# Attention and two mixture layers on one core: half of the strided loads from a second queue

## The chip, the cores and the metric

One core of a Trainium2 chip runs the program. The metric is the device time of one launch in microseconds (us). Before the change the median of three runs is 638.58 us (638.17 to 639.22). A difference under about 0.2% of that, 1.28 us, can't be told from no change here.

## The reference

Three steps, all in float32:

```python
# 1. attention: batch 4, 8 heads, 576 positions, 64 per head
scores = q @ k.T / 8
local   (heads 0-3): rel >= 0 and rel < 32
strided (heads 4-7): rel >= 0 and pos_k % 32 == pos_q % 32
x = softmax(where(mask, scores, -1e9)) @ v         # -> 2304 tokens x 512
# 2. each token goes to the one of 8 experts with the largest cosine:
#    out = gate * (relu(x @ w1[e]) @ w2[e])          (512 -> 1024 -> 512)
# 3. y = max(x @ w1, x @ w2, x @ w3) @ w_out         (512 -> 768 -> 512)
```

## The kernel before

The program is written out in one order by hand; every engine works through its own list, and waits stand on semaphores. The first 124 us are the attention, which also routes the tokens; the remaining 512 us are the experts and the last layer, which TensorE bounds.

The attention takes its work in 44 groups, 11 for each batch: five local groups (kind 0), then six strided ones (kind 1). A strided group is a piece `j` (0 to 2) and a half `hh` (0 or 1), in the order (0,0), (0,1), (1,0), and so on. The strided queries and keys lie in the tiles `qs` and `ks` of 128 partitions x 2 halves x 2 x 576. Half 0 has its data in partitions 0 to 63, half 1 in partitions 64 to 127; the other partitions of each half hold codes that build the mask and are written once, in `setup`. So a group of half 0 needs the loads of partitions 0 to 63 alone, and one of half 1 those of 64 to 127.

The loop in `attention` is a software pipeline over steps `s`. In step `s` the scores of group `s` are issued (`g_scores`, L386), the maximum and the exponentials of group `s-1` (`g_max` L393, `g_exp` L405), the division of group `s-2` (`g_norm`, L417 on GpSimd), the transposes of group `s-4` (L425, copied out by VectorE in L427), a projection of 128 tokens (`tok_half`, L479, copied to `row` in L487 or L489), and the product with the values of group `s-5` (L444, copied out by ScalarE in L454, which the next step issues first). Scores have three buffers in PSUM: group `s` can start when the exponentials of group `s-3` are done.

All loads of the attention are issued by SyncE, one after the other, and SyncE waits where a tile is still being read. Queries and keys of the next kind are asked for by `load_kq` in step 0 or 5 of a batch's 11, the values by `load_v` in steps 4 and 10. For the second to fourth batch the strided ones are asked for at `s` = 11, 22 and 33, when the last strided group of the batch before has been issued; their first group is five steps later, at `s` = 16, 27 and 38. Stores of finished tokens (`x_scr`, L492) go through the same SyncE queue, and so do the weights of the last layer that are re-packed on the way (`c_load`, L213).

Each DMA raises one of eight semaphores, DMAHW0 to DMAHW7, taken in turn. A DMA also waits until the one that used its semaphore before has landed, so at most eight are under way.

Of the kernel before, what the change touches and what calls it, by code (L numbers as in the profile page):

```python
# [69 lines left out]
def kernel(ctx, tc, a, out, x_scr, w_scr, u_scr, perm_scr, gate_scr, upto="all"):  # L70
    nc = tc.nc
# [237 lines left out]
    qs = pa.tile([128, 2, 2, S], F32, name="qs")  # L309
    ks = pa.tile([128, 2, 2, S], F32, name="ks")  # L310
# [14 lines left out]
    def load_kq(b, kind, cuts):  # L325

        for c0, c1, n0, n1 in cuts:
            if kind == 0:
                k0 = n0 + 32 * (n0 > 0)
                nc.sync.dma_start(out=kl[:, c0:c1, k0:n1 + 32], in_=a["ktl"][b][:, c0:c1, k0:n1 + 32])  # L330
                nc.sync.dma_start(out=ql[:, c0:c1, 2 * n0:2 * n1], in_=a["ql"][b][:, c0:c1, 2 * n0:2 * n1])
            else:
                for hh in range(2):
                    h = slice(64 * hh, 64 * hh + 64)
                    nc.sync.dma_start(out=ks[h, hh, c0:c1, n0:n1], in_=a["kts"][b, h, c0:c1, n0:n1])
                    nc.sync.dma_start(out=qs[h, hh, c0:c1, n0:n1], in_=a["qs"][b, h, c0:c1, n0:n1])

    def load_v(b, kind, cuts=((0, 4),)):
        if (b, kind) not in vv:
# [320 lines left out]
    def setup():  # L660
        nc.sync.dma_start(out=masks, in_=a["masks"])
        nc.vector.memset(junk[:, 0:256], 0.0)
        warm(W0, junk)

        nc.scalar.activation(out=junk[:, 1:2], in_=junk[:, 0:1], func=ACTF.Exp)
        for hh, h in enumerate((slice(64, 128), slice(0, 64))):
            for u, (t, eng) in enumerate(((qs, CODE[hh]), (ks, CODE[2 + hh]))):
                shape = [64, 2, 32, 18]
                (nc.gpsimd if eng else nc.vector).tensor_tensor(
                    out=t[h, hh].rearrange("p c (r s) -> p c r s", r=32), op=ALU.add,  # L670
                    in0=bc(code_r[h, u].unsqueeze(1).unsqueeze(3), shape), in1=bc(code_s[h, u].unsqueeze(1).unsqueeze(1), shape))
        load_kq(0, 0, ((0, 1, 0, 256), (0, 1, 256, S), (1, 2, 0, S)))
        nc.sync.dma_start(out=cf, in_=a["cf"][:, 0:308])
        load_v(0, 0, ((0, 2),))
        load_kq(0, 1, ((0, 2, 0, 252),))
        load_v(0, 0, ((2, 4),))
        load_kq(0, 1, ((0, 2, 252, S),))
        nc.sync.dma_start(out=ca, in_=a["cf"][:, 308:])
        nc.sync.dma_start(out=em, in_=a["emb"])
        nc.sync.dma_start(out=tau_c, in_=a["tau"])  # L680
        nc.sync.dma_start(out=cb, in_=a["cb"])
# [544 lines left out]
    with tc.If(over > 0):  # L1226
# [23 lines left out]
        with tc.For_i(0, 16 * E, 1) as j:  # L1250
            val = nc.values_load(tabs[0][0:1, bass.ds(j, 1)], min_val=0, max_val=1)
            with tc.If(val > 0):
# [11 lines left out]
                    out=g, out_offset=None, in_=x_scr, in_offset=bass.IndirectOffsetOnAxis(ap=ids[:, 0:1], axis=0))  # L1264
# [18 lines left out]
                for f in range(6):  # L1283
                    for m in range(3):
                        ps = fpsum("fm")
                        for c in range(4):
                            o = 256 * c + 128 * (f % 2)
                            nc.tensor.matmul(
                                out=ps[:, 0:128], lhsT=wm[:, 3 * (f // 2) + m, o:o + 128], rhs=y2[:, c], start=c == 0, stop=c == 3)
# [5 lines left out]
                for f in range(6):  # L1295
# [5 lines left out]
                    out=out, out_offset=bass.IndirectOffsetOnAxis(ap=ids[:, 0:1], axis=0), in_=fo, in_offset=None)  # L1301
# [89 lines left out]
```

## Time and profile before

| | us |
|---|---|
| median of 3 runs | 638.58 |
| the profiled execution | 638.13 |
| its span, first to last instruction | 636.4 |
| TensorE busy | 610.5 (96%) |
| VectorE busy | 448.9 (71%) |
| ScalarE busy | 336.9 (53%) |
| GpSimd busy | 138.6 (22%) |
| DMA | 130.81 MB, mean 206 GB/s |

A busy engine is not by that the bound: the table is an average over the attention and the two layers, which differ. What a load in the attention is worth has to be read there, from the waits at the groups that use it.

### The profile page before, as it was taken

The page shows a single profiled execution, that of the slowest core. Times are in us where ns is not written, and L with a number is a line of the kernel's source. Part 1 is how long each engine was busy: PE and PEld are TensorE (multiplying, and loading weights), DVE is VectorE, ACT ScalarE, POOL GpSimd, SP SyncE. Part 2 cuts the span into 40 slices and gives each one's busy share as a digit, 9 for nine tenths or more (in the row PEclk, how much of TensorE's full clock was granted, in tenths as well). Part 3 has the DMA queues.
Part 4 walks back from the last instruction along what each step waited for, and adds up shares of the span by engine and source line. Part 5 has one row for each costly group of instructions (what it writes and reads, how often), then busy time and mean ns, then how long its engine had stood idle before and what let it go on. Part 6 is the DMA issues. An engine that isn't in the chain of part 4 may idle for free.

```text
span 636.4 us, 11933 instructions
## 1 busy us (share of the span) xinstructions
PE 610.5 (96%) x4281; PEld 575.7 (90%) x4282; DVE 448.9 (71%) x1011; ACT 336.9 (53%) x909; POOL 138.6 (22%) x133
## 2 busy tenths in 40 slices
PE   7889998799999999999999999999999999999995
PEld 6788887589999999999998999988999988999984
DVE  6868988576899798979899978777344375335440
ACT  3668777555675656566765635546322256221242
POOL 5424443345414142323210000002000012000021
PEclk7999999799999999999999999999999999999998
DMA  8998772584989596878774875931376301377011
GB/s 222 295 227 225 224 195 67 163 285 149 332 285 332 200 347 209 279 239 270 269 249 132 309 305 202 370 154 59 109 268 233 116 33 61 132 269 264 38 49 54
DMA packets 44881, 130.81 MB, mean 206 GB/s; under 512 B 4633, under 2 KB 15513, under 8 KB 41457
## 3 DMA queue, kind: packets, MB, share of 16 engines
q1 hardware_dynamic: 41792, 120.50, 57.1%
q0 software_dynamic: 3024, 9.49, 4.0%
q8 instruction: 36, 0.59, 0.4%
q14 instruction: 29, 0.23, 0.1%
HBM read 97.73 MB, written 32.24 MB: 204 GB/s over the span
## 4 chain that ended last, share of the span: by engine, by line
PE 82%; DVE 7%; DMA 7%; issue 1%; SPq 1%; ACT 1%; POOL 0%; POOLq 0%; DVEq 0%; ACTq 0%
PE g L833 63%; PE q L833 10%; DMA qs<-qs 3%; PE s L386 2%; PE x L444 2%; PE r L479 2%; PE q L816 1%; DMA ks<-kts 1%; DMA out<-r,perm_i 1%; PE t L425 1%; DMA em<-emb 1%; DVE pt L427 1%; DVE mx L393 1%; DMA xg<-x_scr,win_i 1%; DVE tmp L1118 1%
## 5 line engine op out<-in xcount | busy, mean ns | idle before, releaser
L833 PE MATMUL g<-xc,w 128*128 128x384 f32 x1134 | 198.0, 334 | 0.0
L833 PEld LDWEIGHTS g<-xc,w 128*128 128x128 f32 x1134 | 196.5, 188 | 1.2 <-ACT yt L1131 0.5
L178 DVE TENSOR_TENSOR w<-stage,w 128x1024 fp32r<-128x1024 f32 x76 | 104.5, 1391 | 16.5 <-ACT w L173 15.9
L833 PE MATMUL g<-h,w 128*128 128x376 f32 (+7 forms) x768 | 111.6, 301 | 1.5 <-DVE h L853 1.5
L833 PEld LDWEIGHTS g<-h,w 128*128 128x128 f32 x768 | 104.6, 189 | 2.4 <-DVE h L853 1.8
L833 PE MATMUL g<-xw,w 128*128 128x376 f32 (+7 forms) x768 | 106.0, 298 | 0.5 <-ACT xw L808 0.3
L833 PEld LDWEIGHTS g<-xw,w 128*128 128x128 f32 x768 | 104.3, 189 | 0.9 <-ACT xw L808 0.6
L173 ACT ACTIVATE w<-stage 128x1024 fp32r<-128x1024 f32 x76 | 78.7, 1055 | 6.5 <-DMA stage<-w 5.7
L1182 POOL DMA_INDIRECT out<-r,perm_i x18 | 17.9, 994 | 279.3 <-ACT r L1181 197.0
L833 PE MATMUL q<-w,hs 128*128 128x512 f32 x324 | 74.8, 390 | 1.3 <-DVE hs L1170 1.3
L833 PEld LDWEIGHTS q<-w,hs 128*128 128x128 f32 x324 | 60.6, 188 | 14.8 <-DVE hs L1170 2.6
L405 ACT ACTIVATE p<-s,nb 128x96 f32<-128x96 f32 (+2 forms) x152 | 50.7, 346 | 21.7 <-DVE r L414 16.4
L249 POOL TENSOR_TENSOR f<-f,c 128x512 int32<-128x512 int32 x24 | 35.0, 1460 | 108.7 <-DVE f L247 94.4
L1131 ACT ACTIVATE yt<-g 128x384 f32<-128x384 f32 x27 | 13.3, 491 | 72.8 <-PE g L833 40.1
L1118 DVE TENSOR_TENSOR tmp<-g,yt 128x384 f32<-128x384 f32 x36 | 20.0, 555 | 44.7 <-PE g L833 44.7
L417 POOL TENSOR_TENSOR p<-p,ri 128x384 f32<-128x384 f32 (+3 forms) x44 | 36.0, 818 | 60.3 <-DVE ri L416 47.1
L852 ACT ACTIVATE h<-g 128x376 fp32r<-128x376 f32 (+7 forms) x64 | 25.7, 410 | 29.9 <-PE g L833 27.8
L971 DVE TENSOR_TENSOR xc<-yt,xc 128x384 fp32r<-128x384 f32 x42 | 21.4, 553 | 16.4 <-ACT xc L970 16.4
L867 ACT ACTIVATE yt<-g 128x376 f32<-128x376 f32 (+7 forms) x32 | 13.3, 414 | 37.0 <-PE g L833 37.0
L427 DVE COPY pt<-t 96x512 f32<-96x512 f32 (+3 forms) x44 | 25.5, 580 | 8.9 <-PE t L425 8.8
L797 POOL DMA_INDIRECT xg<-x_scr,win_i x22 | 25.8, 1173 | 23.5 <-PE q L947 11.4
L405 ACT ACTIVATION_READ_ACCUMULATOR p<-s,nb 128x1 f32 (+2 forms) x152 | 30.9, 203 | 0.0
(175 smaller groups left out, 793.6 us busy)
## 6 DMA issues: line engine op xcount, KB each, us to landing
stage<-w SPq DMA_DIRECT2D x64, 512.0 KB
c<-wm SPq DMA_DIRECT2D x24, 512.0 KB
w<-u_scr SPq DMA_DIRECT2D x12, 1024.0 KB
u_scr<-w SPq DMA_DIRECT2D x9, 1024.0 KB
w<-u_scr SPq DMA_DIRECT2D x12, 768.0 KB
u_scr<-w SPq DMA_DIRECT2D x9, 768.0 KB
w_scr<-f SPq DMA_DIRECT2D x24, 256.0 KB
stage<-w_scr SPq DMA_DIRECT2D x12, 512.0 KB
```

What stands on the lines that cost most here:

```text
L173: nc.scalar.activation(out=ws[i][:, 0, 0:m], in_=x, func=ACTF.Copy)
L178: nc.vector.tensor_tensor(out=ws[i][:, 1, 0:m], in0=x, in1=ws[i][:, 0, 0:m].bitcast(F32), op=ALU.subtract)
L249: nc.gpsimd.tensor_tensor(out=f, in0=f, in1=low, op=ALU.add)
L405: nc.scalar.activation(out=p[:nq, i, :nk], in_=st[g]["ps"][:nq, i * nk:(i + 1) * nk], func=ACTF.Exp, bias=st[g]["nb"][:nq, i:i + 1], scale ...
L417: nc.gpsimd.tensor_tensor(out=d["p"][:nq, 0:ns, :nk], in0=d["p"][:nq, 0:ns, :nk], in1=ri[:nq, 0:ns].to_broadcast([nq, ns, nk]), op=ALU.mult)
L427: nc.vector.tensor_copy(out=pts[:nk, 0:ns, :nq], in_=pt[:nk, 0:ns * nq].rearrange("p (s q) -> p s q", s=ns))
L797: nc.gpsimd.indirect_dma_start(out=t[i][:r], out_offset=None, in_=x_scr, in_offset=bass.IndirectOffsetOnAxis(ap=win_i[:r, NWIN * e + i:NWI ...
L833: nc.tensor.matmul(out=ps, lhsT=ws(i), rhs=xs(j), start=first and n == 0, stop=last and n == 2, skip_group_check=more)
L852: nc.scalar.activation(out=h[:, 0], in_=ps, func=ACTF.Relu)
L971: nc.vector.tensor_tensor(out=x[:, 1], in0=src[c], in1=x[:, 0].bitcast(F32), op=ALU.subtract)
L1118: nc.vector.tensor_tensor(out=tmps[i], in0=ps, in1=s, op=ALU.add)
L1182: nc.gpsimd.indirect_dma_start(out=out, out_offset=bass.IndirectOffsetOnAxis(ap=perm_i[:, col:col + 1], axis=0), in_=r, in_offset=None)
```

## The change

In the strided branch of `load_kq` the two loops change places, so that both halves of the keys are issued before both halves of the queries. For the second to the fourth batch (`b` above 0) the half of partitions 64 to 127 is issued by ScalarE, in ScalarE's list at the place where `load_kq` is called; the half of partitions 0 to 63 stays with SyncE. For the first batch SyncE issues all four, in the new order. The tiles, the bytes and the shapes of the transfers are the same.

```diff
             else:
-                for hh in range(2):
-                    h = slice(64 * hh, 64 * hh + 64)
-                    nc.sync.dma_start(out=ks[h, hh, c0:c1, n0:n1], in_=a["kts"][b, h, c0:c1, n0:n1])
-                    nc.sync.dma_start(out=qs[h, hh, c0:c1, n0:n1], in_=a["qs"][b, h, c0:c1, n0:n1])
+                for t, x in ((ks, "kts"), (qs, "qs")):
+                    for hh, queue in enumerate((nc.sync, nc.scalar if b else nc.sync)):
+                        h = slice(64 * hh, 64 * hh + 64)
+                        queue.dma_start(out=t[h, hh, c0:c1, n0:n1], in_=a[x][b, h, c0:c1, n0:n1])
```

SyncE's list around the load of the second batch, before. `c` is a weight to re-pack, `v<-vl` the local values, `v<-vs` the strided values, `kl` and `ql` the local keys and queries of the third batch; in brackets the semaphores that are waited for.

```order
L213 DMA c<-wm 128x1024 [waits DMAHW2_49]
L342 DMA v<-vl 96x2304 [waits DMAHW3_49]
L335 DMA ks<-kts 64x1152 [waits DMAHW4_49,PE_49]
L336 DMA qs<-qs 64x1152 [waits DMAHW5_49]
L335 DMA ks<-kts 64x1152 [waits DMAHW6_49,PE_49]
L336 DMA qs<-qs 64x1152 [waits DMAHW7_49]
L342 DMA v<-vs 126x1280 [waits DMAHW0_49]
L330 DMA kl<-ktl 128x1216 [waits DMAHW1_49,PE_49]
```

The first `ks` and `qs` are half 0, the second two half 1. The same stretch of SyncE now:

```order
L213 DMA c<-wm 128x1024 [waits DMAHW2_49]
L342 DMA v<-vl 96x2304 [waits DMAHW4_49]
L336 DMA ks<-kts 64x1152 [waits DMAHW6_49,PE_49]
L336 DMA qs<-qs 64x1152 [waits DMAHW7_49]
L342 DMA v<-vs 126x1280 [waits DMAHW0_49]
L330 DMA kl<-ktl 128x1216 [waits DMAHW1_49,PE_49]
```

The loads of half 0 keep their place behind `c` and `v`; those of half 1 are gone from here. ScalarE's list at the same step, as the difference of the two kernels (`p` are the exponentials, `xt` the copied product with the values):

```order
 L454 ACTIVATE xt<-x 128x128
 L405 ACTIVATE p,rs<-s,nb 72x72 x4
+L336 DMA ks<-kts 64x1152
+L336 DMA qs<-qs 64x1152
 L454 ACTIVATE xt<-x 128x2x14x18
 L405 ACTIVATE p,rs<-s,nb 128x96 x8
```

ScalarE now issues the two loads of half 1 behind the exponentials of the last strided group of the batch before (72x72) and ahead of the next copy `xt`. The same at the third batch:

```order
 L515 ACTIVATE junk,ssq<-row 128x512
 L405 ACTIVATE p,rs<-s,nb 72x72 x2
+L336 DMA ks<-kts 64x1152
+L336 DMA qs<-qs 64x1152
 L515 ACTIVATE junk,ssq<-row 128x512
 L454 ACTIVATE xt<-x 128x2x14x18
```

Here a sum of squares for the routing (L515) and the copy `xt` stand behind the two issues. SyncE in the first batch, second cut of the positions, before:

```order
L342 DMA v<-vl 96x1152 [waits DMAHW5_49]
L335 DMA ks<-kts 64x2x324 [waits DMAHW6_49]
L336 DMA qs<-qs 64x2x324 [waits DMAHW7_49]
L335 DMA ks<-kts 64x2x324 [waits DMAHW0_49]
L336 DMA qs<-qs 64x2x324 [waits DMAHW1_49]
L678 DMA ca<-cf 128x40 [waits DMAHW2_49]
```

In the changed kernel these rows read `ks`, `ks`, `qs`, `qs` with the same waits in the same order: the queries of half 0 move from the second place to the third. TensorE's, VectorE's and GpSimd's lists are unchanged.

## Rows read from the trace of the kernel before

**Rows 1.** The page's part 4, shares of the chain that ended last.

```profile
PE 82%; DVE 7%; DMA 7%; issue 1%; SPq 1%; ACT 1%; POOL 0%; POOLq 0%; DVEq 0%; ACTq 0%
PE g L833 63%; PE q L833 10%; DMA qs<-qs 3%; PE s L386 2%; PE x L444 2%; PE r L479 2%; PE q L816 1%; DMA ks<-kts 1%; DMA out<-r,perm_i 1%; PE t L425 1%; DMA em<-emb 1%; DVE pt L427 1%; DVE mx L393 1%; DMA xg<-x_scr,win_i 1%; DVE tmp L1118 1%
```

**Rows 2.** The chain of waits, 20 to 50 us: start, length, what.

```profile
28.38 16.06 DMA qs<-qs
44.57 1.11 PE s L386 x8
```

**Rows 3.** Windows by stage: us, then busy and (count) per engine, PEclk, DMA share, GB/s.

```profile
44.57:64.00 19.43, 19.43 (x224) 17.63 (x225) 15.77 (x58) 16.03 (x74) 8.37 (x11) 1.00 0.88 242
64.00:124.00 60.00, 52.86 (x607) 45.84 (x607) 51.26 (x204) 43.79 (x191) 21.39 (x27) 0.97 0.55 151
```

**Rows 4.** Timeline, second batch's strided loads and their first two groups: start, length, engine.

```profile
28.38 0.59 SPq L336 DMA_DIRECT2D qs<-qs  x1
29.74 0.35 SPq L342 DMA_DIRECT2D v<-vs  x1
31.38 0.30 ACT L405 ACTIVATE p<-s,nb 72x72 f32<-72x72 f32 x1
32.86 1.05 ACT L454 ACTIVATE xt<-x 128x504 f32<-128x504 f32 x1 [1.08 <-PE x L444]
39.34 0.35 ACT L405 ACTIVATE p<-s,nb 128x96 f32<-128x96 f32 x1
41.63 1.11 PE L386 MATMUL s<-ks,qs 128*126 128x126 f32 x8 [1.48 <-ACT xt L454]
44.57 1.11 PE L386 MATMUL s<-ks,qs 128*126 128x126 f32 x8 [0.31 <-DMA qs<-qs]
```

**Rows 5.** Windows by which transfers are under way, columns as in rows 3.

```profile
25.00:26.00 1.00, 1.00 (x22) 0.76 (x20) 0.68 (x3) 1.00 (x7) 0.83 (x1) 1.00 1.05 440
29.00:30.00 1.00, 0.91 (x7) 0.79 (x8) 0.93 (x6) 0.49 (x4) 0.10 (x1) 1.00 1.02 412
40.00:41.00 1.00, 0.15 (x6) 0.00 (x1) 0.98 (x3) 1.00 (x7) 0.63 (x1) 1.00 0.94 194
42.00:43.00 1.00, 1.00 (x11) 1.00 (x11) 0.00 (x0) 0.14 (x2) 0.79 (x1) 1.00 0.92 212
53.61:65.77 12.16, 12.16 (x133) 10.91 (x131) 10.34 (x45) 10.23 (x47) 5.05 (x8) 1.00 0.95 219
80.19:90.35 10.16, 10.16 (x112) 9.10 (x111) 8.55 (x31) 8.89 (x39) 4.12 (x7) 1.00 0.96 224
```

**Rows 6.** Timeline, third batch: values issued, ScalarE's list, first strided group.

```profile
53.61 0.62 SPq L342 DMA_DIRECT2D v<-vl  x1
57.32 0.31 ACT L405 ACTIVATE p<-s,nb 72x72 f32<-72x72 f32 x1
60.96 0.34 ACT L405 ACTIVATE p<-s,nb 128x96 f32<-128x96 f32 x1 [0.54 <-DVE r L414]
65.77 1.14 PE L386 MATMUL s<-ks,qs 128*126 128x126 f32 x8
```

**Rows 7.** Timeline, fourth batch, the same places and VectorE's copy of a transpose.

```profile
80.19 0.62 SPq L342 DMA_DIRECT2D v<-vl  x1
86.79 0.34 ACT L405 ACTIVATE p<-s,nb 128x96 f32<-128x96 f32 x1 [1.15 <-DVE r L414]
90.35 1.14 PE L386 MATMUL s<-ks,qs 128*126 128x126 f32 x8
91.87 0.61 PE L425 MATMUL t<-cf,p 128*96 128x128 f32 x4 [0.38 <-POOL p L417]
93.64 0.66 DVE L427 COPY pt<-t 96x512 f32<-96x512 f32 x1
```

**Rows 8.** Timeline, first batch: second cut's first strided group, and the next idle time.

```profile
20.17 1.11 PE L386 MATMUL s<-ks,qs 128*126 128x126 f32 x8 [0.25 <-DMA qs<-qs]
23.27 0.69 PE L444 MATMUL x<-pt,v 96*64 96x64 f32 x16 [1.55 <-ACT xt L454]
```

## The prediction

> **What bounds the kernel now.** I read the chain of waits first. TensorE has 82% of it and the DMAs 7%; 73% is line 833, the layers behind the attention [rows 1], which the change does not touch. What the change can move lies in the attention, and one piece there is a load of it: the strided queries of the second batch, issued at 28.38, hold the chain for 16.06 us, until 44.44, and the scores at 44.57 start on that landing [rows 2]. From there to 64 us TensorE is busy 19.43 of 19.43 us [rows 3], so whatever is late at 44.57 is late at 64. From 64 to 124 us VectorE is the fullest of the engines beside TensorE (51.26 and 52.86 of 60 us), and the two feed each other; a delay of one is absorbed only where the other has work in hand.
>
> Then the timeline at the two groups. The first strided group of the second batch (half 0) starts at 41.63 after 1.48 us of idle TensorE [rows 4]. The view names a ScalarE copy, but a score needs no copy: it needs its buffer, which the exponentials of three groups earlier, ended with the row at 39.34, had freed, and its loads. So I take this wait for the landing of half 0, about 41.6. The second group (half 1) starts at 44.57 after only 0.31 us idle, on the landing at 44.44. Between the two lie 2.63 us of TensorE work. The loads thus land one after the other, half 0 first, in the order in which the two groups want them.
>
> Last the windows. While 128-partition loads are under way the queue moves 412 to 440 GB/s; while those of 64 partitions and the values are, 194 to 212; the DMA share is 0.92 to 1.05 in both [rows 5]. The engines of the DMA are busy all the time in either case; in the second they take twice as long for the same bytes.
>
> **The change part by part.**
>
> *The second batch.* SyncE's own issues hardly move: half 0 stays behind the weights and the local values in its queue, and that queue is backlogged. What is new is when half 1 starts. ScalarE reaches its two issues behind the exponentials at 31.38, about 31.8 us, and its queue is empty, so half 1 is served at once, beside the local values that are still in SyncE's queue. Before, 0.59 MB of half 1 (2 transfers of 64 x 1152 x 4 bytes) ran behind half 0; now they run ahead of most of it. If the rate of the two queues together is the 194 to 212 GB/s of the row, the four transfers end when they ended before, but half 0 ends last: at 44.44 in place of 41.6. The first group waits 2.8 us longer. The second finds its data there and follows after the 2.63 us of work: 44.55 + 2.63 = 47.2 in place of 44.57. Cost 2.6 us, all on the path. From the other side: if half 1 slows SyncE's queue not at all, half 0 lands at 41.6 as before and the second group loses its 0.31 us of waiting, a gain of 0.3. The ends are −0.3 and +2.6. I take 2.6, since the nearest rows have the DMA share at 0.92 to 1.05 at the low rate: no DMA engine stands idle that a second queue could put to work.
>
> A rule of the Trainium skill is on the side of that choice. The page "SBUF — State Buffer", section "Can I just issue two DMAs to hit both halves?", says that two concurrent transfers, one at partition 0 and one at partition 64, came to only 6% more than one. No run here shows two such queues yet. By that rule the two pairs of transfers, 2.8 us each, would together take 0.3 us less, and the cost here would be 2.3 in place of 2.6.
>
> *The third batch.* SyncE is held by the token stores until 53.61 and then issues the local values [rows 6]. The last store (0.26 MB), the values (0.88 MB) and half 0 (0.59 MB) are 1.74 MB, at 219 GB/s [rows 5] 7.9 us: half 0 lands near 61.5 and is wanted at 65.77. ScalarE issues half 1 at about 57.8, behind the exponentials at 57.32. Shared rates push half 0 back by its partner's 0.59 MB, 2.7 us, to 64.2, still ahead of the group. The count is a mean over 16 DMA engines, and the last of them ends later, so some wait can appear: 0 to 1.1 us, I take 0.3.
>
> *The fourth batch.* The same count from 80.19 at 224 GB/s gives half 0 at 88.0, and with half 1 ahead of it 90.6; the group starts at 90.35 now [rows 7]. So it waits at least 0.25 and, with a slow last engine, up to 2.6 us. Of that VectorE hides a part: it takes up the transpose of 91.87, ended at 92.48, only at 93.64, so it has 1.16 us of work in hand. Between 0 and 1.5 us reach the path; I take 0.5.
>
> *ScalarE's time.* An issue of such a load takes 0.59 us on SyncE [rows 4], so the pair is about 1.2 us of ScalarE. In the second batch this lies in a gap of 1.08 us, ahead of the copy at 32.86, which waits for TensorE. In the third ScalarE has no gap until 60.96 (0.54 us), in the fourth until 86.79 (1.15 us), and the sum of squares, the copy `xt` and the next exponentials are queued behind the pair; VectorE waits for those exponentials, TensorE's next product for the copy. Cost 0 to 1.2 in each of the two; I take 0.2 each, 0.4 together, since the gap follows within two groups. Would those gaps not be there, it would be 2.4. The new waits of the two loads on earlier DMAs cost nothing: the corresponding loads of SyncE stood behind landings of the same age and were issued by 28.38, before ScalarE arrives.
>
> *The first batch.* The new order puts the queries of half 0 one issue later in each cut. The group at 20.17 already waits 0.25 us for them [rows 8] and will wait about 0.9 longer, one transfer of 0.17 MB at 200 GB/s. It costs nothing, because TensorE is idle 1.55 us before 23.27 anyway, for a copy on ScalarE that stands behind the load of the expert vectors; without that cover it would be the 0.9.
>
> Sum against the profiled execution: 638.13 + 2.6 + 0.3 + 0.5 + 0.4 + 0 = 641.9 us. That execution is 0.45 us under the median of the three runs, well within 0.2%.
>
> **The rivals.**
>
> *The halves help each other.* The 64-partition loads may be slow because their half of the partitions takes no more, and not because the DMA engines are full; then half 1 from a second queue uses the idle other half and SyncE's transfers keep their pace. For it: the same share of busy time at half the rate [rows 5], which says that each packet is slowed at its target. Against it: nothing in the trace shows two queues at work in the attention. Then half 0 lands at 41.6, half 1 long before its group, and the third and fourth batch lose nothing; with ScalarE's issues hidden in its gaps the time is 638.13 − 0.3 = 637.8, not slower. It decides as soon as the two queues together move over about 350 GB/s while both are under way. The Trainium skill, page "SBUF — State Buffer", section "Door 1: The DMA port swizzle", has partitions 0 to 63 and 64 to 127 on different ports, which would be its ground; no row here shows ports.
>
> *Half of that.* If both together move about 300 GB/s, half 1 is done in some 4 us, in which SyncE's queue loses about 1.3 us: half 0 lands at 42.9, a cost of 1.0; the third batch 0, the fourth 0.1, ScalarE 0.2: 639.4.
>
> *ScalarE is the price.* The transfers hide, but each pair of issues falls on the path: 3 x 1.2 = 3.6 us, 641.7. For it: ScalarE is busy 16.03 of 19.43 us [rows 3]. Against it: the gaps named above. The time is near the forecast's, so the place must tell them apart: a late `xt` rather than a late first group.
>
> **How the numbers follow.** Forecast 0.55; the halves help each other 0.20; half of that 0.14; ScalarE's price 0.06; a gain that I can't derive, from a shifted pattern of waits, 0.05. What a measurement here can tell from no change is about 0.2%, 1.28 us, so slower begins at 639.4. Slower: 0.53 of the forecast's 0.55, 0.07 of the half case's 0.14 and 0.06: 0.66. Same: 0.20 + 0.07 + 0.02 = 0.29. Faster 0.05. The forecast's own range is 639.8 to 645.3: the second batch at 1.7, with the rest at 0; and all upper ends together but ScalarE's, 2.8 + 1.1 + 1.5, with 1.8 of ScalarE's 2.4. With the helping case in it the range is 637.5 to 645.
>
> **What would show it.** Right: the first strided group of the second batch starts near 44.5 with some 4 us of idle TensorE ahead of it, the second group has no wait for a load, and the DMA rate from 33 to 44 us stays near 200 GB/s. Wrong: that group still starts near 41.6, or the rate in that stretch exceeds 300, or the copies `xt` behind the new issues start over 1 us late with TensorE idle for them. A time under 639.4 would refute the step of the second batch.

## The result and the profile after

The changed kernel takes 642.32 us (median of 22 runs), the kernel before 639.26 us (22 runs): a ratio of 1.0053, 95% interval 1.0035 to 1.0071, so 3.4 us slower (2.2 to 4.5). The profiled execution of the changed kernel took 646.22 us, 3.9 above its own median. Its attention is some 3 us late; another 5 us come after the attention, where TensorE has the work of before. Single runs of the kernel before differ by as much (637.5 to 642.6 us), so I compare places in the attention and leave the rest to the medians.

First the chain that ended last. Its pieces in the second batch (start, length, what) say which transfer holds it [rows 2]:

```profile
25.66 17.20 DMA qs<-qs
42.86 0.14 issue
42.99 1.61 PE s L386 x8
```

The transfer on the chain was the queries of half 1; now it is those of half 0, issued by SyncE at 25.66 and landed at 42.86. The scores behind it take 1.61 us, before 1.11. The timeline of the same place, ScalarE's rows first, then TensorE's [rows 4]:

```profile
29.14 0.55 ACTq L336 DMA_DIRECT2D ks<-kts  x1
29.81 0.52 ACTq L336 DMA_DIRECT2D qs<-qs  x1
31.54 1.06 ACT L454 ACTIVATE xt<-x 128x504 f32<-128x504 f32 x1 [1.85 <-PE x L444]
...
37.38 0.61 PE L386 MATMUL s<-kl,ql 128*128 128x96 f32 x4
42.99 1.61 PE L386 MATMUL s<-ks,qs 128*126 128x126 f32 x8 [4.16 <-DMA qs<-qs]
47.15 1.14 PE L386 MATMUL s<-ks,qs 128*126 128x126 f32 x8
```

ScalarE's two issues fit into its gap: the next copy `xt` waits for TensorE. The first strided group waits 4.16 us in place of 1.48, the second not at all. From group to group it is 4.16 us, though the work between them took 2.63 before. The windows of the changed kernel (us, busy and count per engine, PEclk, DMA share, GB/s) show why [rows 5]:

```profile
33.00:44.00 11.00, 6.84 (x71) 6.22 (x70) 6.05 (x22) 6.60 (x36) 3.31 (x4) 0.98 1.01 201
40.00:41.00 1.00, 0.00 (x0) 0.00 (x0) 0.35 (x2) 0.81 (x5) 0.36 (x1) 1.00 1.07 237
44.00:45.00 1.00, 1.00 (x6) 0.98 (x6) 0.00 (x0) 0.00 (x0) 0.00 (x0) 0.50 0.95 225
46.00:47.00 1.00, 1.00 (x18) 0.75 (x17) 0.97 (x4) 0.00 (x0) 0.00 (x0) 0.57 0.95 397
```

and the first of these stretches in the kernel before:

```profile
33.00:44.00 11.00, 9.52 (x106) 8.77 (x106) 7.26 (x26) 7.92 (x39) 3.73 (x5) 1.00 0.99 195
```

Two readings. With two queues the DMAs move 201 GB/s where one moved 195, at a share of 1.0 in both: a second queue brings no more that can be told. (The same stretch has 196 to 205 GB/s in six profiles that load half of the second batch from ScalarE, this one and five from below, and 195 to 239 in six that load all of it from SyncE; the 3% lie far inside that spread.) And after the 4.16 us without work TensorE's granted clock is 0.50, the level of 1.2 GHz, until it is back near 47 us: that is the long work between the groups, 4.16 − 2.63 = 1.5 us.

When half 1 moves can be read too. Of the DMA queues q10 appears only in kernels in which ScalarE loads; q1 is SyncE's. The first row below is the stretch from 34 to 36 us, the next two that from 36 to 42 (packets, MB, share of the 16 engines), the last the time from issue to landing of ScalarE's queries:

```profile
q10 hardware_dynamic: 2, 0.01, 2.6%
...
q1 hardware_dynamic: 160, 0.71, 55.1%
q10 hardware_dynamic: 150, 0.58, 44.5%
...
qs<-qs ACTq DMA_DIRECT2D x1, 288.0 KB, 14.1
```

ScalarE issues at 29.14 and 29.81, but from 30 to 34 us q10 moves nothing; nearly all of half 1's 0.59 MB goes from 36 to 42, side by side with SyncE's bytes. Its queries land at 29.81 + 14.1 = 43.9, a microsecond behind half 0's 42.86. TensorE reaches the second group only at 47.15, so it finds them there.

From 47 to 67 us TensorE is again busy throughout, as in [rows 3], so nothing of the delay is given back:

```profile
47.15:66.60 19.45, 19.45 (x228) 17.66 (x225) 15.55 (x55) 16.20 (x74) 8.16 (x11) 1.00 0.68 180
```

The third and fourth batch: ScalarE's first issue and the second strided group of the third, then the first two of the fourth [rows 6, 7]:

```profile
59.76 0.48 ACTq L336 DMA_DIRECT2D ks<-kts  x1
...
72.01 1.11 PE L386 MATMUL s<-ks,qs 128*126 128x126 f32 x8 [0.21 <-DMA qs<-qs]
...
94.10 1.11 PE L386 MATMUL s<-ks,qs 128*126 128x126 f32 x8 [0.87 <-issue]
96.89 1.15 PE L386 MATMUL s<-ks,qs 128*126 128x126 f32 x8
```

The second group of each batch is the clean place to compare, since the waits of the first lie ahead of it. In the kernel before, the last local group ahead of the second batch's and the second groups of the third and fourth batch:

```profile
38.70 0.61 PE L386 MATMUL s<-kl,ql 128*128 128x96 f32 x4
...
69.11 1.15 PE L386 MATMUL s<-ks,qs 128*126 128x126 f32 x8
...
94.03 1.14 PE L386 MATMUL s<-ks,qs 128*126 128x126 f32 x8
```

Before, the second groups started at 44.57, 69.11 and 94.03; now they start 2.58, 2.90 and 2.86 us later. Nearly all of the attention's delay arises in the second batch, in this execution.

### The profile page after: what moved, and what is told of

It reads as the page before. It is cut to its first block, busy times and chain, and to the rows that moved or that the text cites. A ratio compares the mean times of both kernels' runs of the same rounds, so it can differ in the third digit from the quotient of the medians.

```text
span 644.4 us, 11937 instructions
## 1 busy us (share of the span) xinstructions
PE 613.0 (95%) x4281; PEld 577.4 (90%) x4282; DVE 449.2 (70%) x1011; ACT 337.6 (52%) x909; POOL 138.1 (21%) x133
## 4 chain that ended last, share of the span: by engine, by line
PE 77%; DMA 11%; DVE 9%; issue 1%; ACT 1%; SPq 0%; POOL 0%; POOLq 0%; DVEq 0%; ACTq 0%
PE g L833 59%; PE q L833 10%; DMA qs<-qs 4%; PE s L386 2%; PE r L479 1%; PE q L816 1%; DMA cf<-cf 1%; PE x L444 1%; DMA out<-r,perm_i 1%; DMA kl<-ktl 1%; DMA ks<-kts 1%; DVE pt L427 1%; DMA xg<-x_scr,win_i 1%; DVE w L178 1%; DMA stage<-w 1%
## 5 line engine op out<-in xcount | busy, mean ns | idle before, releaser
L833 PE MATMUL g<-h,w 128*128 128x376 f32 (+7 forms) x768 | 113.4, 304 | 1.5 <-DVE h L853 1.5
L833 PEld LDWEIGHTS g<-h,w 128*128 128x128 f32 x768 | 106.3, 192 | 2.7 <-DVE h L853 2.0
L405 ACT ACTIVATE p<-s,nb 128x96 f32<-128x96 f32 (+2 forms) x152 | 50.7, 348 | 19.2 <-DVE r L414 14.1
```

The lines of the kernel that those rows point to most:

```text
L405: nc.scalar.activation(out=p[:nq, i, :nk], in_=st[g]["ps"][:nq, i * nk:(i + 1) * nk], func=ACTF.Exp, bias=st[g]["nb"][:nq, i:i + 1], scale ...
L833: nc.tensor.matmul(out=ps, lhsT=ws(i), rhs=xs(j), start=first and n == 0, stop=last and n == 2, skip_group_check=more)
```

## The experiments

My theory: the second queue brings no more bytes, half 0 lands late, TensorE waits, and its clock falls on top. The rivals: ScalarE's issues are the price; the first batch's new order is what matters; every batch pays. All ratios are to the kernel before, run on the same chip in turn.

| kernel | ratio | 95% interval |
|---|---|---|
| new order in the first batch only | 0.9963 | 0.9940 to 0.9987 |
| second batch only | 1.0036 | 1.0007 to 1.0066 |
| third and fourth only | 1.0077 | 1.0046 to 1.0109 |
| halves swapped between the queues | 1.0116 | 1.0080 to 1.0153 |
| ScalarE's issues, without the bytes | 1.0023 | 0.9994 to 1.0051 |
| new order, one queue | 1.0005 | 0.9976 to 1.0034 |
| changed kernel, 14 filling products | 1.0082 | 1.0048 to 1.0116 |
| third batch only | 1.0088 | 1.0058 to 1.0117 |
| first and second batch | 1.0042 | 1.0014 to 1.0070 |
| third only, ScalarE's queue used earlier | 1.0018 | 0.9991 to 1.0044 |
| changed kernel, 6 filling products | 1.0043 | 1.0013 to 1.0073 |
| first batch only, re-packing later | 0.9995 | 0.9976 to 1.0014 |

In the diffs, `new(b)` stands for the changed loop, `old` for that of before.

**The parts, each alone.**

```diff
-new(b) for every b
+new(b) if b == 0 else old
```

> The new order of the four loads (keys of both halves, then queries of both halves) in the first batch alone, all from SyncE; batches two to four as before. The prediction put this at nothing: 0 us against the kernel before. Rival: the changed kernel's profile is 2.1 us early at the load of the expert vectors and 1.3 us early at 40 us, and if the new order is the cause this kernel is 1 to 2 us faster than before (ratio 0.997 to 0.9985) and its first strided group of the second batch starts near 40.3.

Measured: 0.9963, about 2.4 us faster, against my 0. Two more kernels below have the same order in the first batch, and they show 1.0005 and 0.9995. One interval of three excludes no change; I take the gain as not settled.

```diff
-new(b) for every b
+new(b) if b == 1 else old
```

> ScalarE issues half 1 in the second batch alone; first, third and fourth batch as before. Theory of the late half 0: the whole cost is here, +3 to +4.3 us (ratio 1.005 to 1.007), the first strided group of the second batch starts near 44.5 after about 4 us of idle TensorE. Rival, the issues on ScalarE are the price: a third of the cost, +1 us, with that group near 41.6.

Measured: 1.0036, 2.3 us. The first two strided groups of the second batch:

```profile
41.35 1.11 PE L386 MATMUL s<-ks,qs 128*126 128x126 f32 x8 [1.09 <-DMA qs<-qs]
45.51 1.11 PE L386 MATMUL s<-ks,qs 128*126 128x126 f32 x8 [1.53 <-DMA qs<-qs]
```

Here half 0 costs no more than before (1.09 us of waiting, before 1.48) and half 1 is late: the second group starts 0.94 us later than before. ScalarE reached its issues at 31.33 in this execution, in the changed kernel's at 29.14. So one of the halves is late here too, but the other one; that this goes with ScalarE's later start is my reading, and no run varies it alone.

```diff
-new(b) for every b
+new(b) if b > 1 else old
```

> ScalarE issues half 1 in the third and fourth batch alone; first and second batch as before. Theory of the late half 0 in the second batch: no cost, -0.3 to +0.5 us (ratio 0.9995 to 1.0008). The prediction's own terms for these batches are +1.2 us. Rival, ScalarE's issues: two thirds of the cost, +2 us (ratio 1.003).

Measured: 1.0077, 4.9 us. My theory of these two batches missed by far. ScalarE's first issue, and TensorE's first two strided groups of the fourth batch:

```profile
56.20 3.41 ACTq L336 DMA_DIRECT2D ks<-kts  x1
```

```profile
93.85 2.04 PE L386 MATMUL s<-ks,qs 128*126 128x126 f32 x8 [1.75 <-DMA qs<-qs]
98.02 1.14 PE L386 MATMUL s<-ks,qs 128*126 128x126 f32 x8
```

An issue that took 0.48 us in the changed kernel takes 3.41 here, with the sum of squares and the copy `xt` queued behind it. In the fourth batch half 0 is late by 1.75 us, and the group's 8 products take 2.04 us in place of 1.14, at the lower clock. The second groups of this execution's second and third batch:

```profile
43.54 1.18 PE L386 MATMUL s<-ks,qs 128*126 128x126 f32 x8 [0.45 <-DMA qs<-qs]
...
70.84 1.14 PE L386 MATMUL s<-ks,qs 128*126 128x126 f32 x8
```

It enters the third batch 1.03 us ahead of the kernel before (43.54 against 44.57). From second group to second group it takes 27.30 us (before 24.54), and to that of the fourth 27.18 (before 24.92): losses of 2.8 and 2.3 us, 5.0 together, as the medians have it.

**The halves change queues.**

```diff
-SyncE loads half 0, ScalarE half 1
+SyncE loads half 1, ScalarE half 0   (b > 0; b == 0: old)
```

> As the change for batches two to four, but with the halves exchanged: ScalarE issues half 0, which the first strided group needs, SyncE half 1; the first batch in the old order. Theory of the late half: half 0 lands by 40 us, the first strided group of the second batch starts without a wait near 40.2, half 1 lands near 44.4 as before and the second group starts near 44.6 after about 1.8 us of idle TensorE; no cost, -0.5 to +0.5 us (ratio 0.999 to 1.001). Rival, ScalarE's issues or a slower rate of two queues together: +3 us as the change (ratio 1.005).

Measured: 1.0116, 7.4 us, against no loss. The first two strided groups of the second and of the third batch:

```profile
45.08 2.04 PE L386 MATMUL s<-ks,qs 128*126 128x126 f32 x8 [3.44 <-DMA qs<-qs]
49.87 1.43 PE L386 MATMUL s<-ks,qs 128*126 128x126 f32 x8
...
75.32 2.04 PE L386 MATMUL s<-ks,qs 128*126 128x126 f32 x8 [3.88 <-DMA qs<-qs]
80.10 1.66 PE L386 MATMUL s<-ks,qs 128*126 128x126 f32 x8
```

ScalarE's queue starts later than SyncE's (30.08 against 26.71 for the second batch's first issue), and now it carries the half that is wanted first. Both batches wait 3.4 to 3.9 us for it, and in both the clock falls behind the wait: from group to group it is 4.8 us (before 2.9 in the second batch, 3.3 in the third). The profiled execution, 650.49 us, is the slowest of six, so its places show the kind of loss and not its size.

**ScalarE's issues without the bytes.**

```diff
 SyncE: old, but half 1 without its last 16 positions (b > 0)
+ScalarE: ks and qs of half 1, last 16 of 576 positions, where new(b) issues
```

> The loads keep the order and the queue they had before, but the last 16 of the 576 positions of half 1 are loaded by ScalarE, at the places where the change puts its loads: six more issues on ScalarE, almost no bytes in its queue. It asks which part of the change's loss is ScalarE's time. If the loss of the third and fourth batch (4.9 us when these alone were changed) is made of ScalarE's issues, this kernel loses it too, and some of it in the second batch: 3 to 6 us, a ratio of 1.005 to 1.009. If the loss is made of half 0 landing later, because half 1 runs beside it, this kernel loses the 0 to 1.2 us of three pairs of issues: a ratio of 1.000 to 1.002. I expect 1.001.

Measured: 1.0023, an interval that holds 0 and the 1.2 us of the issues, and whose upper end, 3.3 us, is nearly the change's whole loss. The ratio alone doesn't settle it; the trace says more. The first strided groups of the second, third and fourth batch (this kernel's line numbers are three higher):

```profile
40.30 1.11 PE L389 MATMUL s<-ks,qs 128*126 128x126 f32 x8 [0.30 <-DMA qs<-qs]
...
64.44 1.14 PE L389 MATMUL s<-ks,qs 128*126 128x126 f32 x8
...
89.01 1.14 PE L389 MATMUL s<-ks,qs 128*126 128x126 f32 x8
```

They lie 1.33, 1.33 and 1.34 us ahead of those before (41.63, 65.77, 90.35). The lead doesn't shrink over the second and third pair of issues. The first pair, at 31.09 and 31.83, lies ahead of these groups: the local groups on either side of it start at 29.73 and 38.56, before at 29.82 and 38.70, so it costs nothing either, and the lead comes from a load that landed earlier (a wait of 0.30 us in place of 1.48). On the path the issues cost nothing in this execution.

**The new order in one queue.**

```diff
-for hh, queue in enumerate((nc.sync, nc.scalar if b else nc.sync)):
+for hh, queue in enumerate((nc.sync, nc.sync)):
```

> All four loads of every batch stay with SyncE, in the new order: both halves of the keys, then both halves of the queries. ScalarE issues nothing. The queries of half 0 are now third of four, so half 0 ends about 1.4 us (one transfer of 0.29 MB at 200 GB/s) later than before, not 2.8. If the late half 0 is the price, the second batch loses about 1.4 us, the third and fourth next to nothing, and the first batch's order gains its 2.4: about 1 us under before, a ratio of 0.996 to 1.000. If the price is a second queue or ScalarE, nothing is lost: 2 to 2.5 us under before, a ratio of 0.996. The two lie close; the wait of the first strided group of the second batch tells them apart, near 43 us in the first case, near 39.3 in the second.

Measured: 1.0005. The first two strided groups of the second batch:

```profile
40.77 1.14 PE L386 MATMUL s<-ks,qs 128*126 128x126 f32 x8
43.63 1.14 PE L386 MATMUL s<-ks,qs 128*126 128x126 f32 x8
```

Neither waits for a load. So the order alone is not the loss, and the 1.4 us that I gave it did not appear. The second queue, with the waits of the issues that it shifts, is all that differs from the changed kernel, and the intervals of the two (up to 1.0034, from 1.0035) don't overlap: the loss goes with the second queue.

**The first and second batch together.**

```diff
-new(b) for every b
+new(b) if b < 2 else old
```

> The new order in the first batch and ScalarE's queue in the second, as in the change; the third and fourth batch as before. Changed alone, the first batch gained 2.4 us, the second lost 2.3 and the third (with or without the fourth) 5. In the profile of the changed kernel, though, the third and fourth batch lost nothing. If that holds, this kernel stands where the change stands, 3.4 us over before, a ratio of 1.005, because the second batch's landing swallows the first batch's gain: it is a fixed time that does not move with what is ahead of it. If the parts simply add up, it is 0 us over before and the third batch carries the loss, a ratio of 1.000. I expect 1.004.

Measured: 1.0042, 2.7 us, against the change's 3.4: most of the change's loss is here, as expected. Its second batch repeats the changed kernel's to 0.2 us:

```profile
42.85 2.04 PE L386 MATMUL s<-ks,qs 128*126 128x126 f32 x8 [3.87 <-DMA qs<-qs]
...
47.00 1.15 PE L386 MATMUL s<-ks,qs 128*126 128x126 f32 x8
```

**The third batch.**

```diff
-new(b) for every b
+new(b) if b == 2 else old
```

> ScalarE's queue for the third batch alone, everything else as before. The kernel that changed the third and the fourth lost 4.9 us. If each batch pays for its own late half, the third, where the profile of that kernel showed no wait for the load but an issue of 3.4 us on ScalarE with TensorE idle 1.35 us for the copy behind it, loses 1 to 2 us and the fourth, where TensorE waited 1.75 us for the load and the clock fell, the other 3: a ratio of 1.002 to 1.003. If the long issue is the rule and the larger part, 4 us: 1.006. If it was one execution's chance, within 0.5 us: 1.000 to 1.001.

Measured: 1.0088, 5.6 us: the long issue again, and the larger part. ScalarE's issue:

```profile
55.14 4.42 ACTq L336 DMA_DIRECT2D ks<-kts  x1
```

and on TensorE the first strided group of the second batch, the product that waits for the copy, and the first strided group of the third:

```profile
39.70 1.11 PE L386 MATMUL s<-ks,qs 128*126 128x126 f32 x8 [0.27 <-DMA qs<-qs]
...
61.94 1.95 PE L444 MATMUL x<-pt,v 126*64 126x126 f32 x16 [2.37 <-ACT xt L454]
...
67.70 1.14 PE L386 MATMUL s<-ks,qs 128*126 128x126 f32 x8
```

Between the two groups it is 28.00 us; before it was 24.14 (41.63 to 65.77). The product behind the wait takes 1.95 us in place of 1.08: here too the clock falls (0.50 from 62 to 65 us).

```diff
 new(b) if b == 2 else old
+b == 1: ScalarE loads the last 16 positions of half 1
```

> ScalarE's queue for the third batch alone, but in the second batch ScalarE already loads the last 16 positions of half 1 (almost no bytes). In the two kernels that first used ScalarE's queue in the third batch its first issue held ScalarE 3.4 and 4.4 us; in five that had used it in the second batch it took 0.5 us there. If the long issue belongs to a first use in that place and makes the third batch's loss of 5 us, it is gone here: 0 to 1.5 us over before, a ratio of 1.000 to 1.002. If the loss is the late half or the second queue as such, it stays at 4 to 5 us: 1.007.

Measured: 1.0018, an interval apart from that of the kernel above. The issue of the keys, and the first strided group of the second and the third batch:

```profile
58.13 0.50 ACTq L337 DMA_DIRECT2D ks<-kts  x1
```

```profile
42.59 1.11 PE L389 MATMUL s<-ks,qs 128*126 128x126 f32 x8 [0.98 <-DMA qs<-qs]
...
66.71 1.14 PE L389 MATMUL s<-ks,qs 128*126 128x126 f32 x8
```

0.50 us in place of 4.42, and 24.12 us between the groups, as before the change. So the third batch's loss, 3.9 us between the groups in the one profile, goes with the long issue. That came in the two kernels in which ScalarE's queue is first used in the third batch; the changed kernel doesn't have it. Why it is long stays open: the extra loads also shift the semaphores on which the issues wait.

**The clock.**

```diff
-g_scores(s)
+(warm(14) if s == 16 else None, g_scores(s))    # products that nothing reads
```

> The changed kernel with 14 products on no data that matters, issued by TensorE ahead of the first strided group of the second batch, where it is idle 4.16 us in the profile after. If the fall of the granted clock to 0.50 behind that wait costs something by itself, it goes: the two groups behind the wait take 2.6 us each as before in place of 4.16 for the first, 1.5 us less than the changed kernel, a ratio to before of about 1.003. If the fall costs nothing on the path, or the clock falls all the same, the ratio stays at 1.005. The load lands at the same time in either case.

Measured: 1.0082, not better than the change. The filling and the two groups behind it:

```profile
39.54 6.31 PE L499 MATMUL warm<-cf 128*128 128x256 f32 x28
45.69 1.04 PE L386 MATMUL s<-ks,qs 128*126 128x126 f32 x8
...
48.18 1.14 PE L386 MATMUL s<-ks,qs 128*126 128x126 f32 x8
```

I sized it wrongly: 6.31 us run past the landing (42.86 in the changed kernel's profile), and the group starts when they end. But behind it the two groups are 2.49 us apart in place of 4.16.

```diff
-warm(14) if s == 16
+warm(6) if s == 16
```

> The changed kernel with 6 filling products ahead of the second batch's first strided group in place of 14: some 2.7 us in place of 6.3, so that they end before the load lands. In the profile with 14 the granted clock stayed at 1.00 and the group behind took 2.5 us in place of 4.16, but the products ended 2.7 us after the load would have landed. If that clock is what costs, this kernel is 1.5 us under the change: a ratio to before of 1.003. If 6 are too few to hold the clock or it costs nothing, 1.005.

Measured: 1.0043. The second batch, then the first strided group of the fourth:

```profile
39.78 2.86 PE L499 MATMUL warm<-cf 128*128 128x256 f32 x12
42.48 1.04 PE L386 MATMUL s<-ks,qs 128*126 128x126 f32 x8
...
44.96 1.14 PE L386 MATMUL s<-ks,qs 128*126 128x126 f32 x8
```

```profile
92.57 1.74 PE L386 MATMUL s<-ks,qs 128*126 128x126 f32 x8 [1.30 <-DMA qs<-qs]
96.73 1.15 PE L386 MATMUL s<-ks,qs 128*126 128x126 f32 x8
```

In the second batch the price of the clock is gone: 2.48 us between the groups. The median is 0.6 us under the change's by the ratios, with intervals that overlap, so the 1.5 us are shown in the trace and not in the time. In the fourth batch this execution waits 1.30 us for half 0, and the groups are 4.16 us apart at the lower clock. So does the one with 14 products: it waits 2.16 us there, and its groups too are 4.16 us apart.

**What stands ahead of the load.**

```diff
 first batch's new order only
-S0 = 6     # step at which the weights to re-pack are asked for
+S0 = 17
```

> The new order in the first batch alone (0.9963), and the two weights to re-pack (1 MB), which stand ahead of the second batch's strided loads in SyncE's queue, asked for eleven groups later. If the second batch's strided loads land late because of what stands ahead of them, they land up to 4 us earlier and the wait there goes; in the profile with the new order that wait is down to 0.17 us, so little is left to gain: 0 to 0.5 us, a ratio of 0.995 to 0.996. If the late re-packing delays the stores or the third batch's loads, 1 to 3 us are lost.

Measured: 0.9995, no gain from it. In its profile neither of the second batch's first two groups waits for a load. Of all versions the new order in the first batch alone is the fastest measured (0.9963), but since its two relatives stand at 0.9995 and 1.0005, I don't call it shown.

## Why the prediction was right

The forecast was 641.9 us, measured were 642.32. Part of that nearness is luck: the forecast adds 3.8 us to an execution of 638.13, and in the rounds of the result the kernel before had a median of 639.26; the change cost 3.4. Taken step by step it is less exact still.

*The second batch, +2.6.* The core is shown: two queues together no faster than one, half 0 late, a first group with 4.16 us of idle time, a second group that finds its data. One step under it was wrong. I had half 1 "served at once", from about 31.8 us, ahead of most of half 0, so that half 0 would end last. Its bytes moved from 36 to 42 us beside SyncE's, some 5 us and more behind ScalarE's issues, and half 0 landed a microsecond ahead of half 1. As I read these rows, half 0 is late because the two halves share the engines while both move; no run varies that alone. Why ScalarE's bytes start so late is open.

The second group starts 2.58 us later than before. But that number is a sum that I hadn't written: 2.68 for the longer wait (4.16 − 1.48), −0.31 for the wait that went, +1.53 for the lower clock, which the prediction left out, and −1.32 because this execution came to the place earlier (the last local group starts at 37.38, before at 38.70). With that lead the landing at 42.86 is where I had put it, 44.44 − 1.32 = 43.1. The kernel with the first and second batch alone, 2.7 us slower, bears out the size; the term that is missing and the lead happened to cancel. A single profile can't carry the size: in two kernels that are as before up to there (the third and fourth batch alone, the third alone) the second group starts at 43.54 and 42.55, not at 44.57. What separates the kernels is TensorE's wait at the second batch's first two groups. It is 2.6 to 4.2 us in the four profiles with half 1 or half 0 on ScalarE and no filling products (the change 4.16, first and second batch 3.87, swapped 3.44, second batch only 2.62), and 0 to 1.8 us in the eight without, two of them with the last 16 positions on ScalarE.

The Trainium skill (page "SBUF — State Buffer", section "Can I just issue two DMAs to hit both halves?") has two concurrent transfers at only 6% over one. The traces agree in that two queues bring next to nothing, 201 against 195 GB/s, but can't tell 6% from none.

*The third batch, +0.3.* 0.32 in the profile (2.90 − 2.58), but it is half 1 that is late, by 0.21 us, not half 0. The test of this batch alone cost 5.6 us, most of which goes with the long issue that the changed kernel doesn't have.

*The fourth batch, +0.5.* Nothing in the changed kernel's profile (2.86 against 2.90): TensorE is idle for 0.87 us ahead of the first group, for a reason that the profile doesn't show, and makes it up before the second. In three other profiles whose fourth batch is loaded as in the change half 0 is 1.30 to 2.16 us late and the clock falls. From the second group of the third batch to that of the fourth it was 24.92 us before; it is 26.69 with the 6 filling products (70.04 to 96.73), 27.18 in the kernel of these two batches alone (70.84 to 98.02) and 27.57 with the 14 products (72.75 to 100.32), losses of 1.8 to 2.7 us. So the profile of the changed kernel is the mild case here, and its median may hold some of this. My bound of 1.5 left the clock out here too. The 0.7 us between the change and the kernel without its third and fourth batch lie inside the intervals.

*ScalarE, +0.4.* Not told from 0 by the ratio, nor from 3 us (1.0023, 0.9994 to 1.0051); the trace shows no cost. As the place test of the rival asked, no copy `xt` is late behind the issues in the changed kernel. The rival is not dead in general: one issue of 3.4 to 4.4 us cost a kernel 5.

*The first batch, 0.* Open: −2.4, −0.3 and +0.3 us by the three kernels that have the order without the second queue (the last has it in every batch).

*The rivals of two halves that help each other* needed 300 to 350 GB/s. The stretch has 201, and its best microsecond ahead of half 0's landing 237. (In the case of half the help, 300 GB/s shared evenly over 3.9 us leave SyncE 1.0 us behind, not 1.3; nothing hangs on it.)

*The range.* Its ends use 1.7 and 2.8 us for the second batch, which the working, with −0.3 and +2.6, doesn't give; the time lies inside either way.

## What to carry to other kernels

Here, at a DMA share near 1.0, a second queue brought no more bytes; it only changed which transfer ends when, and the one wanted first came later. Before adding a queue ask which transfer is wanted first, and what the new one will run beside. Price a wait of TensorE with the clock behind it: 2.7 us of longer waiting cost another 1.5. Read more than one profile: programs that are the same up to a place reached it up to 2 us apart. A part tested alone can have a cost that it doesn't have in the whole, so test the combinations too.

## What was unexpected of the hardware

- TensorE's granted clock fell to 0.50 around the end of the second batch's waits of 3.4 to 4.2 us, for 3.4 us in the changed kernel and for over 6 us with the halves swapped, and the 2.63 us of work between its two groups took 4.15 to 4.79. It was also at the lower level behind waits of 1.30, 1.75 and 2.16 us in the fourth batch, and not behind the 1.48 us of [rows 4] or the 1.53 us of the second batch alone.
- Loads that ScalarE issued at 29.14 and 29.81 us moved no byte from 30 to 34 us and nearly all of theirs from 36 to 42, while SyncE's queue had work all along.
- A DMA issue on ScalarE took 3.41 and 4.42 us in the two kernels that first used that queue in the third batch, 0.48 to 0.55 us there in the six kernels that had used it in the second. The second batch's own first issue took 0.55 to 0.66 us.
- One load's landing, not the work ahead of it, set the second batch's start: with two queues the first group started at 42.85 and 42.99 in two kernels, though their work had reached the place 3.9 and 4.2 us before.
